# Spectral gate beside a feed-forward block: the opening as one written-out list, and three real products per complex product in half of the transform over s

## The chip, the cores and the metric

One core of a Trainium2 chip runs the whole program. The metric is device time in microseconds, the median of several executions. PE is TensorE (matmuls), PEld its weight loads, DVE VectorE, ACT ScalarE, POOL GpSimd, SP SyncE, whose queue issues most DMAs.

## What is computed

```python
def reference(A_x, A_w_r, A_w_i, B_x, B_w1, B_w2):      # x: 1 x 2048 x 1024
    xn = _layernorm(A_x, axis=-1)
    X = jnp.fft.rfft2(xn, axes=(-2, -1)) * (A_w_r + 1j * A_w_i)
    s = jnp.fft.irfft2(X, s=(2048, 1024), axes=(-2, -1))
    h = _silu(xn @ B_w1)                                 # 1024 x 3584
    g = _silu(h @ B_w2)                                  # 3584 x 1024
    return A_x + s * g
```

Two parts share the normalized input: a feed-forward block of two large products, and a two-dimensional Fourier transform with a filter in the frequency domain. The last line joins them.

## The kernel before

Everything that goes through PE is float32 split into two float16 halves, `hi` and `lo`, and a product is the sum of three: hi x hi, hi x lo, lo x hi. The high half is an ACT copy (`high`, line 253) and the low half a DVE subtraction (`low`, line 256).

**The first FFN product** (`mm1`, line 449) makes, for a block `c` of 512 positions (four blocks) and a tile `f` of 128 hidden columns (28 tiles), 24 matmuls of 512 columns into one PSUM tile of the tag "ff" (four of them). Its stationary operand is the weight tile `w1t[f]`, its moving operand the transposed normalized block `xnT[c]`. Before a weight tile can be used it is loaded (`load`), its largest absolute value per row taken (`maxi`), those summed over the partitions by a tiny matmul (`column_sums`, line 260), a power of two derived from the sum (`scales`), and the halves made (`split`, `rest`). The weight tiles 0 and 1 share one sum, and so do 2 and 3.

**The second FFN product** (`mm2`, line 537) runs as seven products `m` of block sums and differences, each in eight steps `j`; a step is 42 matmuls of 512 columns (9 us).

**The spectral part** is done between these, as background. `ln_gen` normalizes and transposes; block 0 by matmuls (`trans`), the others by transposing DMAs (`entering`, `turned`). `fa_mat` and `fd_gen` transform along the model dimension and do the first radix-4 steps along positions; the results, real and imaginary planes `v`, go to DRAM as `vd`, split in halves (`high_r`, `low_r`). `f_gen` (line 935) then runs 16 units `u`, with `q = u // 4` and `j = u % 4`. For each unit PE multiplies the planes by cosine and sine matrices `kq` (`mat`, line 958): with cosine 128x256 on both planes, with sine and minus sine 128x128 crosswise, for four `c` and three halves each, 36 matmuls into one PSUM tile of the tag "ft" (two of them). ACT copies half of it (`copy`, line 984), DVE forms sum and difference straight from PSUM (lines 1015 and 1016), does a radix-4 step, multiplies with the filter (1030, 1031, 1043, 1044) and does the radix steps of the inverse (1047 to 1066, a small share on POOL). The result is split (`high_z`, `low_z`) and stored as `zd` when four units are done; the tile `zq` is then taken again, so the high half after it waits for that store. `edge_gen` (line 1074) does the same for the one column left over: 12 POOL copies (1089 to 1092), 18 tiny float32 matmuls into a tile "eps" (1096 to 1098), small POOL products. `i_gen` transforms back (1215, 1223, 1305) and writes the rows of `s` (last at 1352) that `finish_out` uses.

**The order.** Each engine works its instructions in the order in which this program issues them. After each half of a product step, `work` (line 1458) takes up to three steps of the background queue `bg` as long as a count of DVE time, kept by `meter` from instruction sizes, is not more than 1 us ahead of the same count for PE. A generator's `yield` ends a step. The edge job stands in that queue behind the 16 units, and behind it the switch to the inverse transform. The opening is ordered by hand: `WARM` gives numbers of idle matmuls (`spin`) between the steps, and the strings `ENTRY` say, for the first five products, after which third of the matmuls how many steps of which queue are issued (`w` weights, `b` background, `f` and `e` the transform matmuls and evacuations of block 0).

Of the kernel before, what the change touches and what calls it, by code (L numbers as in the profile page):

```python
# [2 lines left out]

# [6 lines left out]
F16 = mybir.dt.float16  # L10
# [12 lines left out]
WARM = [35, 8, 0, 8, 0, 8, 12, 0, 0, 0, 0]  # L23
LEAD, PAUSE, LAST = 1.0, -1, 6
IORDER = (1, 3, 0, 2)
SUMMED = (4, 5)
TURNED = (2, 3)
EXTRA = (20, 22, 24)
ENTRY = ("fbwb||ew", "bbbwwbb|bwbb|f", "fwwbbw|wbbb|wb", "|wew|wf", "w||w")
# [15 lines left out]
def make_constants():  # L45
# [16 lines left out]
    k = np.stack([-np.sin(th), np.cos(th), np.sin(th)], 3)  # L62
    kc = np.stack(_halves(k, 2.0**14), 3).reshape(4, 128, 3072)
# [65 lines left out]
def spectral_ffn(ctx, tc, x, w_r, w_i, w1, w2, ca, kc, ci, tw, pm, out):  # L129
# [19 lines left out]
    vd = [dp.tile([128, 4, 4, 2, 256], F16, name=f"vd{j}") for j in range(4)]  # L149
    zd = [dp.tile([128, 4, 2, 1024], F16, name=f"zd{c}") for c in range(4)]  # L150
# [96 lines left out]
    e1, m1, r1, rs, s1 = (small(k, NFT) for k in ("e1", "m1", "r1", "rs1", "s1"))  # L247
# [10 lines left out]
    m1b = sm.tile([128, NFT], BF16, name="m1b")  # L258

    def column_sums(name, m, n, ones=ones):  # L260
        ps = pf.tile([128, 512], F32, name=name, tag="ff")
        nc.tensor.matmul(ps[:, 0:n], ones, m, start=True, stop=True)
        return ps[:, 0:n]

    def weights1():
# [11 lines left out]
        def maxi(i):  # L277
            nc.vector.tensor_reduce((m1 if i < 6 else m1b)[:, i:i + 1], raw[i], axis=AX.XY, op=OP.max, apply_absolute_value=True)

        def scales(i, k):  # L280
            sl = slice(i, i + k)
            ps = column_sums(f"s1_{i}", *((m1[:, sl], k) if i < 6 else (m1b[:, sl], k, unit)))
# [21 lines left out]
        for i in range(3):  # L304
            load(i)
        yield 0

        def first(i):

            maxi(i)  # L310
            if i == 0:
                load(3)

        def whole(i):

            split(i)
            if i in (1, 3):
                load(4 + i // 2)

        steps = {"m": first, "s": lambda i: scales(i, 1), "p": lambda i: scales(i, 2), "h": whole, "l": rest}  # L320
        for k in "m0 m1 p0 h0 l0 h1 l1 m2 m3 p2 h2 l2 h3 l3 m4 s4 h4 l4 m5 s5 h5 l5".split():
            steps[k[0]](int(k[1]))
            yield 0
# [125 lines left out]
    def mm1(c, f, between={}):  # L449
        ps = pf.tile([128, 512], F32, name=f"pa{c}_{f}", tag="ff")  # L450
        w, xt = w1t[f], xnT[c]
# [3 lines left out]
        for n, (d, wh, xh) in enumerate(terms):  # L455
            if n in between:
                between[n]()
            nc.tensor.matmul(ps, w[:, wh, d], xt[:, xh, d], start=(n == 0), stop=(n == 23))  # L458
# [238 lines left out]
    def entering(c, stats, norm):  # L697
# [23 lines left out]
        steps = {"s": stats, "n": plain, "h": hi, "l": lo}  # L721
        for k in "s0 s1 n0 h0 n1 l0 h1 s2 l1 s3 n2 h2 n3 l2 h3 l3".split():
            steps[k[0]](int(k[1]))
            yield 0

    def ln_gen(c):
# [33 lines left out]
        if c == 0:  # L760
            for p in range(2):
                stats(p)
                norm[p]()
            trans(0)
            hi(0)
            stats(2)
            norm[2]()
            trans(1)
            hi(1)
            stats(3)  # L770
            norm[3]()
            lo(0)
            yield 0
            trans(2)
            hi(2)
            lo(1)
            yield 0
            trans(3)
            hi(3)
            lo(2)  # L780
            yield 0
            lo(3)
            yield 0
            return
        yield from (turned if c in TURNED else entering)(c, stats, norm)
# [20 lines left out]
    def fd_gen(c):  # L806
# [62 lines left out]
        o, sp = {}, {}  # L869

        def high_r(j):
            sp[j] = ap.tile([128, 4, 2, 256], F16, name=f"Rs{c}_{j}", tag="Rs", bufs=2)
            nc.scalar.activation(sp[j][:, :, 0], o[j], AF.Copy, scale=2.0**-21)

        def low_r(j):
            nc.vector.scalar_tensor_tensor(sp[j][:, :, 1], o[j], 2.0**-21, sp[j][:, :, 0], op0=OP.mult, op1=OP.subtract)
            defer(2, lambda: nc.sync.dma_start(vd[j][:, :, c], sp[j]))

        for j in range(4):
# [11 lines left out]
            o[j] = r.rearrange("a (q r) k -> a q (r k)", r=2)  # L891
            yield 3.9
# [36 lines left out]
    def open_f():  # L929
        J["p"] = ctx.enter_context(tc.tile_pool(name="jit", bufs=1, side="right"))  # L930
        B["es"] = ExitStack()
        B["p"] = B["es"].enter_context(tc.tile_pool(name="flt", bufs=1, side="right"))
        B["k"], B["v"], B["w"], B["z"] = {}, {}, {}, {}

    def f_gen():
# [12 lines left out]

        def load_w(u):
# [8 lines left out]
        def mat(u):  # L958
            q = u // 4
            ps = pt.tile([128, 4, 2, 128], F32, name=f"fx{u}", tag="ft")  # L960
            v, k = B["v"].pop(u), B["k"][q]
# [22 lines left out]
        def copy(u):  # L984
            cps[u] = bp.tile([128, 2, 256], F32, name=f"xc{u}", tag="xc", bufs=1)
# [21 lines left out]
        for u in range(16):  # L1007
# [3 lines left out]
            ps, cpy = psx.pop(u), cps.pop(u)  # L1011
            pv = ps.rearrange("m c r k -> m c (r k)")
            b = bp.tile([128, 2, 2, 128], F32, name=f"xb{u}", tag="xb", bufs=1)
            d = bp.tile([128, 2, 2, 128], F32, name=f"xd{u}", tag="xd", bufs=1)
            tt(b.rearrange("m c r k -> m c (r k)"), pv[:, 0:2], cpy, op=OP.add)
            tt(d.rearrange("m c r k -> m c (r k)"), pv[:, 0:2], cpy, op=OP.subtract)
# [5 lines left out]
            i_, n_, q_ = u // 8, u // 4 % 2, u % 4  # L1022
# [623 lines left out]
```

## Time and profile before

| | |
|---|---|
| median of 3 runs | 1229.07 us (1228.78, 1229.07, 1231.65) |
| the profiled execution | 1231.15 us, its span 1229.4 us |
| matmuls | 6992, each with a weight load |
| PE busy | 1218.5 us, 99% of the span |
| DVE busy | 999.7 us, 81% |
| ACT busy | 471.5 us, 38% |
| first matmul of the first FFN product | at 19.06 us |
| units of `f_gen` | about 570 to 840 us |
| inverse transform's first matmul | at 892.34 us |

A timeline row gives the start, the duration, engine, line, operation, what it writes and reads, the shape and a count of merged instructions; in brackets stands how long the engine had been idle and what ended that. A matmul's duration contains its latency: 512 columns show as 0.38 us but follow one another every 0.216 us. A row of the waits gives who waited for whom, total, times and longest, in us. A row of one tile or line gives shortest, median and longest duration in ns and the first and last start.

### The profile page before, as it was taken

What the parts mean: (1) busy time and instruction counts of PE and PEld (TensorE: products, weight loads), DVE (VectorE), ACT (ScalarE), POOL (GpSimd) and SP (SyncE); (2) the same over time, 40 slices, a digit from 0 to 9 for tenths busy, and PEclk for the clock granted to TensorE, in tenths of its full rate; (3) what the DMA queues carried; (4) which work ended last, traced back from release to release, by engine and by line L of the source; (5) the groups of instructions that cost most, each with busy time, mean ns of one, the idle gap of its engine ahead of it and who ended that gap; (6) DMA issues with size and microseconds to landing.
All of it is one profiled execution on the core that took longest, in us unless ns stands there. A gap on an engine that the chain in (4) does not pass through costs nothing.

```text
span 1229.4 us, 19034 instructions
## 1 busy us (share of the span) xinstructions
PE 1218.5 (99%) x6992; PEld 619.8 (50%) x6992; DVE 999.7 (81%) x1974; ACT 471.5 (38%) x614; POOL 119.7 (10%) x247
## 2 busy tenths in 40 slices
PE   8999999999999999999999999999999999999998
PEld 5544445444544454445445555544455545555545
DVE  7778998799899889887969899885186678798885
ACT  6675343343554555435433222122032222233212
POOL 3320000000000000010001121114111111000000
PEclk9999999999999999999999999999999999999999
DMA  8887477645669797759899989987979999998686
GB/s 250 186 199 182 139 235 218 202 131 166 201 188 299 226 296 225 217 188 285 178 301 236 299 249 192 276 243 244 285 195 286 276 291 331 305 355 327 199 268 253
DMA packets 279550, 295.77 MB, mean 241 GB/s; under 512 B 48544, under 2 KB 207264, under 8 KB 279072
## 3 DMA queue, kind: packets, MB, share of 16 engines
q1 hardware_dynamic: 259440, 235.76, 65.6%
q10 hardware_dynamic: 15984, 51.45, 12.2%
q0 software_dynamic: 4032, 7.34, 3.5%
q8 instruction: 55, 0.90, 0.3%
q14 instruction: 39, 0.32, 0.1%
HBM read 185.95 MB, written 102.25 MB: 234 GB/s over the span
## 4 chain that ended last, share of the span: by engine, by line
PE 70%; DVE 11%; DMA 8%; issue 3%; ACT 3%; POOL 0%; SPq 0%; ACTq 0%; DVEq 0%; POOLq 0%
PE pa L458 41%; PE pb L541 8%; PE pb L543 8%; PE pb L542 8%; DVE Z L1066 2%; DMA zd<-zq 2%; PE id L1305 2%; DVE T L1031 1%; ACT xp L740 1%; DMA sd<-s 1%; DVE w L256 1%; PE iu L1215 1%; DMA ht<-hd_sum_d 1%; DMA wq<-in_A_w_i_dram 1%; DVE zq L997 1%
## 5 line engine op out<-in xcount | busy, mean ns | idle before, releaser
L458 PE MATMUL pa<-xnT,w 128*128 128x512 f16 x2688 | 584.1, 379 | 1.2 <-ACT w L253 0.7
L458 PEld LDWEIGHTS <-w 128*128 128x128 f16 x2688 | 261.4, 98 | 313.1 <-issue 1.2
L541 PE MATMUL pb<-w,ht 128*128 128x512 f16 (+2 forms) x812 | 301.2, 373 | 0.0
L543 PE MATMUL pb<-w,ht 128*128 128x512 f16 (+2 forms) x812 | 301.0, 373 | 0.0
L542 PE MATMUL pb<-w,ht 128*128 128x512 f16 (+2 forms) x812 | 301.0, 372 | 0.0
L543 PEld LDWEIGHTS <-ht 128*128 128x128 f16 x812 | 79.6, 98 | 91.5 <-issue 0.8
L542 PEld LDWEIGHTS <-ht 128*128 128x128 f16 x812 | 79.6, 98 | 87.1 <-issue 0.8
L541 PEld LDWEIGHTS <-ht 128*128 128x128 f16 x812 | 79.6, 98 | 87.0 <-issue 0.6
L467 ACT ACTIVATE h<-pa,s 128x512 f32<-128x512 f32 x112 | 75.8, 678 | 117.6 <-PE pa L458 94.1
L253 ACT ACTIVATE w<-jr,sc 128x512 f16<-128x512 f32 x98 | 68.1, 713 | 84.4 <-DMA jr<-in_B_w_dram 35.9
L253 ACT ACTIVATE hosum<-hr,hs 128x1536 f16<-128x1536 f32 x28 | 44.1, 1574 | 78.3 <-DVE hr L497 41.4
L256 DVE SCALAR_TENSOR_TENSOR w<-jr,sc,w 128x512 f16<-128x512 f32 x98 | 71.1, 744 | 2.7 <-ACT w L253 2.7
L253 ACT ACTIVATE hoone<-h,hs 128x2048 f16<-128x2048 f32 x28 | 56.0, 1999 | 44.6 <-issue 26.5
L256 DVE SCALAR_TENSOR_TENSOR hoone<-h,hs,hoone 128x2048 f16<-128x2048 f32 x28 | 65.6, 2344 | 7.1 <-ACT hoone L253 7.1
L992 ACT ACTIVATE zq<-Z,zs 128x1024 f16<-128x1024 f32 x16 | 18.4, 1148 | 99.1 <-DVE Z L1066 50.9
L256 DVE SCALAR_TENSOR_TENSOR hosum<-hr,hs,hosum 128x1536 f16<-128x1536 f32 x28 | 50.8, 1813 | 2.5 <-ACT hosum L253 2.5
L496 DVE TENSOR_TENSOR hr<-h 128x1024 f32<-128x1024 f32 x28 | 34.2, 1222 | 22.8 <-ACT h L467 22.8
L634 ACT ACTIVATE pl<-pl,c 128x512 f32<-128x512 f32 (+2 forms) x28 | 17.4, 656 | 67.9 <-DVE pl L610 39.1
L965 PE MATMUL fx<-vq,kq 128*128 128x256 f16 x192 | 43.2, 273 | 0.0
L253 ACT ACTIVATE w<-w1r,rs 128x1024 f16<-128x1024 f32 x28 | 31.9, 1144 | 29.0 <-DVE w L256 19.1
L966 PE MATMUL fx<-vq,kq 128*128 128x128 f16 x192 | 42.0, 219 | 0.0
L967 PE MATMUL fx<-vq,kq 128*128 128x128 f16 x192 | 42.0, 219 | 0.0
(225 smaller groups left out, 1514.0 us busy)
## 6 DMA issues: line engine op xcount, KB each, us to landing
w1r<-in_B_w_dram SPq DMA_DIRECT2D x28, 512.0 KB, 6.5
hd_sum<-hosum SPq DMA_DIRECT2D x56, 256.0 KB, 2.9
hd_one<-hoone SPq DMA_DIRECT2D x56, 256.0 KB, 3.7
hd_dif<-hoone SPq DMA_DIRECT2D x56, 256.0 KB, 3.2
w2m<-in_B_w_dram SPq DMA_DIRECT2D x28, 512.0 KB, 6.2
ht<-hd_dif ACTq DMA_DIRECT2D x32, 448.0 KB, 6.2
jr<-in_B_w_dram SPq DMA_DIRECT2D x56, 256.0 KB, 6.9
ht<-hd_sum ACTq DMA_DIRECT2D x32, 448.0 KB, 5.9
```

The lines of the kernel that those rows point to most:

```text
L253: nc.scalar.activation(hi, raw, AF.Copy, scale=scale)
L256: nc.vector.scalar_tensor_tensor(lo, raw, scale, hi, op0=OP.mult, op1=OP.subtract)
L458: nc.tensor.matmul(ps, w[:, wh, d], xt[:, xh, d], start=(n == 0), stop=(n == 23))
L467: nc.scalar.activation(hq[:, 2 * (c % 2) + f % 2], ps, AF.Silu, scale=s1[:, f:f + 1])
L496: tt(sums[:, 0:2], hq[:, 0::2], hq[:, 1::2], op=OP.subtract)
L541: nc.tensor.matmul(ps, hh[:, 0], w[:, 0], start=first, stop=False)
L542: nc.tensor.matmul(ps, hh[:, 0], w[:, 1], start=False, stop=False)
L543: nc.tensor.matmul(ps, hh[:, 1], w[:, 0], start=False, stop=last)
L965: nc.tensor.matmul(o, k[:, c, kh, 1], v[:, c, vh], start=(n == 0), stop=False)
L966: nc.tensor.matmul(ps[:, c, 0], k[:, c, kh, 2], v[:, c, vh, 128:256], start=False, stop=False)
L967: nc.tensor.matmul(ps[:, c, 1], k[:, c, kh, 0], v[:, c, vh, 0:128], start=False, stop=(n == 2))
L1066: eng.tensor_tensor(Z[:, ns, pos], x0[:, :, ls], x1[:, :, ls], op=o_)
```

## The change

1. The opening is one list of operations by name. `S N T H L` are the statistics, normalization, transposes and halves of block 0's four parts, `A B X Y` the same for block 1, `M s C h l` a weight tile's maximum, column sum, scale and halves, `W` idle matmuls, `f e` transform matmuls and evacuations, `v` a first product's evacuation. `P` and `Q` mark the points within the products up to which the list is issued. The weight tiles 0 to 3 get a sum and scale each; all sums use the bfloat16 matrix. Weight tile 0 is loaded ahead of the third and fourth x tile.
2. The very first product is made in two halves of 256 columns, first the one that needs parts 0 and 1 of the block only.
3. For `q` in (2, 3), the units 8 to 15, a complex product is three real ones: cos (vr + vi), (sin - cos) vi and (-sin - cos) vr, 36 matmuls of 128 columns. `fd_gen` makes and stores the sums vr + vi. The unit's result lies in two "ft" tiles; ACT copies the common product twice over (both planes) and DVE adds the other two to it.
4. The edge job is run inside the units: its loads two a unit from the first unit on, its copies behind unit 13, its matmuls in unit 14, in an "ff" tile.

```diff
-WARM = [35, 8, 0, 8, 0, 8, 12, 0, 0, 0, 0]
+WARM = 35
+THREE = (2, 3)
-ENTRY = ("fbwb||ew", "bbbwwbb|bwbb|f", "fwwbbw|wbbb|wb", "|wew|wf", "w||w")
+ENTRY = (
+    "S0 S1 M0 N0 s0 N1 C0 S2 h0 T0 H0 S3 L0 T1 W12 H1 L1 N2 T2 W4 N3 T3 H2 H3 l0 P0ah A0 L2 L3 P0ax M1 "
+    "P0al P0b0 B0 f0 A1 X0 s1 P0b1 f1 C1 M3 e0 P0b2 M2 f2 h1 A2 s3 s2 v0e B1 Y0 C2 e1 X1 h2 P1b0 l1 P1b1 "
+    "f3 B2 P1b2 C3 P2b0 Y1 P2b1 A3 l2 h3 X2 Y2 P2b2 B3 l3 P3b0 M4 s4 X3 Y3 C4 v1e h4 v2e P3b1 P3b2 v3e Q0 "
+    "Q1 l4 Q2 "
+)
...
+    k[list(THREE)] = np.stack([np.cos(th), np.sin(th) - np.cos(th), -np.sin(th) - np.cos(th)], 3)[list(THREE)]
...
     def mm1(c, f, between={}):
+        parts = ((0, 256), (256, 512)) if c + f == 0 else ((0, 512),)
...
+        for b, (first, stop) in enumerate(parts):
+            for n, (d, wh, xh) in enumerate(terms):
+                if 24 * b + n in between:
+                    between[24 * b + n]()
+                nc.tensor.matmul(
+                    ps[:, first:stop], w[:, wh, d], xt[:, xh, d, first:stop], start=(n == 0), stop=(n == 23))
...
+            both[j] = ap.tile([128, len(THREE), 2, 128], F16, name=f"vt{c}_{j}", tag="wd", bufs=3)
+            nc.scalar.activation(both[j][:, :, 0], total[j], AF.Copy, scale=2.0**-21)
...
+            nc.vector.scalar_tensor_tensor(both[j][:, :, 1], total[j], 2.0**-21, both[j][:, :, 0], op0=OP.mult, op1=OP.subtract)
+            defer(2, lambda: nc.sync.dma_start(vs[j][:, :, c], both[j]))
...
+            nc.vector.tensor_tensor(total[j], some[:, :, 0:128], some[:, :, 128:256], op=OP.add)
+            clock["dve"] -= 0.8
...
         def mat(u):
+            if q in THREE:
+                t_ = B["s"].pop(u)
+                for half in range(2):
+                    ps = pt.tile([128, 2, 512], F32, name=f"fx{u}_{half}", tag="ft")
+                    for i, c in enumerate((half, half + 2)):
+                        for g, src in enumerate((t_[:, c], v[:, c, :, 128:256], v[:, c, :, 0:128])):
+                            for n, (kh, vh) in enumerate(((0, 0), (0, 1), (1, 0))):
+                                nc.tensor.matmul(ps[:, i, 128 * g:128 * g + 128], k[:, c, kh, g], src[:, vh], start=(n == 0), stop=(n == 2))
+                    psx[u, half] = ps
+                return
...
         def copy(u):
+            if u // 4 in THREE:
+                cps[u] = bp.tile([128, 2, 2, 2, 128], F32, name=f"xo{u}", tag="T1", bufs=1)
+                for half in range(2):
+                    nc.scalar.activation(cps[u][:, half], psx[u, half][:, :, 0:128].unsqueeze(2).broadcast_to([128, 2, 2, 128]), AF.Copy)
+                return
...
+            if q in THREE:
+                for half in range(2):
+                    planes = psx.pop((u, half))[:, :, 128:384].rearrange("m i (r k) -> m i r k", r=2)
+                    tt(cpy[:, half], cpy[:, half], planes, op=OP.add)
+                pv = cpy.rearrange("m h i r k -> m i h (r k)")
+                pv, cpy = pv[:, 0], pv[:, 1]
...
+            if u == 12:
+                B["edge"] = edge_gen()
...
+            if u > 12:
+                next(B["edge"], None)
...
-        ps = pt.tile([128, 1024], F32, name="eps", tag="ft")
+        ps = pf.tile([128, 512], F32, name="eps", tag="ff")
...
-                add(bg, edge_gen())
```

Lines 1028 to 1062 of the old loop got `next(B["edge"])` at further steps of units 12 to 15, one step of the edge job each. The filter weights, the number of units and the inverse transform are the same.

216 lines of the change are left out of this document (115 added, 101 removed).

## The prediction

> **What bounds the kernel now.** I read the page's busy line first, then the busy time by stretch, then TensorE's (PE's) waits, and then the timeline wherever one of those three showed a hole.
>
> ```profile
> PE 1218.5 (99%) x6992; PEld 619.8 (50%) x6992; DVE 999.7 (81%) x1974; ACT 471.5 (38%) x614; POOL 119.7 (10%) x247
> ```
> ```profile
> 45.00:1224.70 1179.70, 1178.01 (x6709) 593.85 (x6706) 962.40 (x1908) 438.76 (x582) 105.40 (x209) 1.00 0.82 241
> ```
> ```profile
> PE eps L1096 <- POOL edge L1089: 0.7, 1, 0.7
> PE eps L1098 <- POOL edge L1092: 0.2, 1, 0.2
> ```
>
> The second view's columns are the stretch, its length, then busy time of PE, PEld (weight load), DVE (VectorE), ACT (ScalarE) and POOL (GpSimd), granted clock, DMA share, GB/s. Its stretch from 45 us to 1224.7 us has PE busy 1178.01 of 1179.70 us, so the span is a start, a solid block of matmuls and a short tail. The third view shows all that PE waits for between 560 and 850 us, the spectral units among it: the small edge product, 0.9 us. So a change can win only by streaming fewer columns, by starting the first product sooner, or by mending the edge product; and it loses whatever new wait it gives PE. That DVE is 81% busy costs nothing until PE has to wait for it.
>
> **The units' matrices.** A unit's transform before, and narrow matmuls elsewhere:
>
> ```profile
> 700.00 0.27 PE L965 MATMUL fx<-vq,kq 128*128 128x256 f16 x1
> 700.11 0.22 PE L966 MATMUL fx<-vq,kq 128*128 128x128 f16 x1
> ...
> 702.65 0.38 PE L541 MATMUL pb<-w,ht 128*128 128x512 f16 x1
> ```
> ```profile
> 892.34 2.84 PE L1215 MATMUL iu<-kk,zt 128*128 128x128 f16 x48
> ```
> ```profile
> 22.14 5.34 PE L458 MATMUL pa<-xnT,w 128*128 128x512 f16 x24
> ```
>
> One unit holds PE from 700.00 to 702.65, 2.65 us for 36 matmuls (12 of 256 columns, 24 of 128). After the change it is 36 of 128 columns, each still with its own weight load. What such a stream costs is in the second row: 48 in 2.84 us, the last one's 0.22 being latency, so 2.62 / 47 = 55.7 ns each. 36 x 55.7 ns = 2.01 us; saved 0.64 a unit, and 8 units give **-5.1 us**, all on PE and so all on the path.
>
> Against this change speaks the Trainium skill, "TensorE: Matmul & The Clock Gate", section "Back-to-back issue gap": in a real stream of weight load and matmul it has a 128-column matmul cost some 81 ns, not the isolated 56. By that a unit would take an estimated 2.92 us and the eight units would cost 2.1 us more than now. The trace doesn't bear it out: its 48 narrow matmuls, each with a load, run at 55.7 ns.
>
> The first product in halves is 48 matmuls of 256 columns in place of 24 of 512. By the 0.11 us from 700.00 to 700.11 they take 5.28 us, against (5.34 - 0.38) / 23 = 0.216, so 5.18 us: **+0.1 us**. Fewer warm-up matmuls save nothing by themselves, as they only fill time in which PE has no data.
>
> **The opening.** ACT, DVE, SP (SyncE's queue) and PE:
>
> ```profile
> 7.72 2.58 ACT L740 ACTIVATE x<-x,v 128x1024 f32<-128x1024 f32 x2 [5.50 <-POOL v L739]
> 10.21 1.02 ACT L753 ACTIVATE xnT<-tp 128x1024 f16<-128x1024 f32 x1
> ...
> 17.86 2.19 ACT L253 ACTIVATE w<-w1r,rs 128x1024 f16<-128x1024 f32 x2 [0.77 <-DVE rs L286]
> ```
> ```profile
> 12.41 1.21 DVE L278 TENSOR_REDUCE m<-w1r 128x1 f32<-128x1024 f32 x1
> ...
> 17.06 0.16 DVE L283 TENSOR_SCALAR e<-s 128x2 int32<-128x2 int32 x1
> ```
> ```profile
> 3.07 6.54 SPq L275 DMA_DIRECT2D w1r<-in_B_w_dram  x3
> ```
> ```profile
> DMA to landing us min/median/max: 8.5/9.6/10.1
> ```
> ```profile
> 14.90 1.13 PE L749 MATMUL tp<-ident,x 128*128 128x128 f32 x8 [0.25 <-DVE xnT L757]
> ...
> 19.06 1.90 PE L458 MATMUL pa<-xnT,w 128*128 128x512 f16 x8 [0.71 <-ACT w L253]
> ```
>
> The first product starts at 19.06, released by the first weight tile's high half, which ACT could begin only at 17.86: the scale, whose first step is the 17.06 row, came out of two maxima and a joint column sum. The weight tile itself landed at 3.07 + 8.5 = 11.6. In the new list it is loaded ahead of the third and fourth x tile, and its maximum, sum and scale are taken alone. One tile earlier by two transfers (the three weight tiles land some 1.8 us apart) is 8.6 or so; 1.21 of maximum and about 1.1 of sum and scale give 10.9. From there ACT is the chain: high half 1.1 (2.19 for two), two xnT tiles 2.0, two normalizations 2.6, so 16.6; the last tile's transposes, 1.1 in the 14.90 row, are ahead of the product on PE, and two hand-overs, hence a start near 18.0: **-1.1 us**. Bounds: if the two later x tiles' statistics set it, ACT waits about a microsecond and nothing is won; with no wait for DMA at all ACT has no gap and it is -2. The pieces behind (second scale, second high half, transposes of the second x block) each have a transform or a half product ahead of them on PE; I leave **+0.4** for a wait among the column sums, which stand on PE behind DVE's maxima, with 0 and 1.5 as ends.
>
> **The edge product.** Now it runs alone behind the last unit:
>
> ```profile
> 836.95 0.38 PE L543 MATMUL pb<-w,ht 128*128 128x512 f16 x1
> 838.01 0.40 PE L1096 MATMUL eps<-edge,perm 128*128 128x24 f32 x2 [0.68 <-POOL edge L1089]
> ...
> 840.13 0.38 PE L1096 MATMUL eps<-edge,perm 128*128 128x24 f32 x2
> ...
> 840.80 0.38 PE L541 MATMUL pb<-w,ht 128*128 128x512 f16 x1
> ...
> 842.01 0.63 PE L542 MATMUL pb<-w,ht 128*128 128x512 f16 x1
> 842.44 0.63 PE L543 MATMUL pb<-w,ht 128*128 128x512 f16 x1
> ```
> ```profile
> 700.00:840.00 140.00, 139.01 (x861) 75.41 (x860) 128.70 (x237) 29.85 (x42) 24.61 (x52) 1.00 0.89 233
> 840.00:890.00 50.00, 50.00 (x229) 22.81 (x230) 12.20 (x18) 7.54 (x12) 14.15 (x43) 0.97 0.99 290
> ```
>
> PE was due at 837.17 and is back on the main product at 840.80: 3.63 us. The last six matmuls, with nothing to wait for, take 0.67, so 18 take 2.0 and 1.6 are waits for POOL's 12 copies. Then matmuls of 512 columns come 0.43 us apart instead of 0.216, and the stretch from 840 to 890 has a granted clock of 0.97, which over 50 us is some 3 us at half speed: 1.6 us more. The change issues the copies behind unit 13 and the matmuls two slots later, in unit 14. If the copies are done by then, 1.6 is won; whether the half clock comes all the same I take as even, 0.8: **-2.4 us**. Ends: -3.2 with both gone, and +3.4 where PE waits for unit 13 to finish (first rival). The Trainium skill's section "Part 1: The HAM clock gate" in the same page says that the clock is judged in free-running windows of 3.4 us; the 0.43 us spacing agrees with its half rate. By that, 2.0 us of tiny matmuls without a wait would seldom fill a window.
>
> **What DVE, ACT and the tiles get.**
>
> ```profile
> DVE zq L997 <- ACT zq L992: 14.4, 3, 8.5
> ```
> ```profile
> L1016 DVE TENSOR_TENSOR xd<-fx,xc 128x512 f32<-128x512 f32 x10 | 6.8, 676 | 0.0
> ```
> ```profile
> 811.85 0.27 PE L965 MATMUL fx<-vq,kq 128*128 128x256 f16 x1
> ```
> ```profile
> 813.22 0.68 DVE L1016 TENSOR_TENSOR xd<-fx,xc 128x512 f32<-128x512 f32 x1
> ```
> ```profile
> L1352 DVE SCALAR_TENSOR_TENSOR rows<-sk,spa x4: 282/283/285, 1166.3 to 1191.7; 128x128 f32<-128x128 f32 x4
> ```
> ```profile
> L876 DVE SCALAR_TENSOR_TENSOR Rs<-Ro,Rs x16: 1212/1218/1226, 155.9 to 547.5; 128x1024 f16<-128x1024 f32 x16
> ```
>
> Each changed unit has two more adds of 128x512: 2 x 0.68 = 1.36 us, 10.9 in all; ACT copies twice instead of once. In the forward part 16 steps get an add and a split of 256 elements: by a quarter of 1.218 at least, by half of 0.676 plus an issue at most, 0.6 to 0.9 together, about 13 us spread over 400; there the diff takes 0.8 us back from the planner's count, so the order stays as it is and DVE's idle fifth takes it. Neither is on PE. The planner counts the unit's adds (its meter sees every DVE instruction), so units come out further apart and the last ones move into 840 to 890, where DVE works 12.2 of 50 us; the edge steps that stood there now ride inside the units. The inverse transform's last rows are at 1191.7 and their last use is the final product, which ends at 1224.7: 33 us of cover for a delay of at most 24. If that cover were gone, the tail would grow by the excess. The new 128 KB stores and 256 KB loads are issued two units ahead like their neighbours; the small edge loads go two per unit in the first eight on SP's queue, in front of those units' weight loads, and the permutation's load moves from unit 14 to 12. On POOL the edge's copies and small sums now stand among the Z steps of units 13 to 15, for which ACT's high halves wait; a delay there reaches DVE, not PE, and falls in the idle stretch.
>
> What is new for PE is the PSUM tile. Before, a unit took one of the two "ft" tiles, so its matrix had a whole unit's grace. Now a unit takes both, and the next unit's matrix waits until DVE's two adds have read them. The last unit shows how near that is: its matrix starts at 811.85, while DVE finishes reading the unit before at 813.90. The adds stand ahead of that reading and would release the tiles some 0.7 us earlier, so this one would have waited 1.4 us. Seven such hand-overs; lower end 0, upper end in the second rival. I take **+1.0**, one late hand-over like this one, since only this unit comes behind DVE's 8.5 us wait. ACT's copies for the next unit write the buffer that DVE's last product of this unit still reads, so they come later than now; DVE's eight Z steps cover them. The edge product's tile is one of the four of the main product, free again after ACT's next copy. Behind a waiting matrix stands the whole second FFN product, so such a wait is paid in full.
>
> **Sum:** -5.1 + 0.1 - 1.1 + 0.4 - 2.4 + 1.0 = -7.1 us. The profiled execution took 1231.15 us (span 1229.4), 2.1 above the median of 1229.07; part of that may be its half clock, so against the median I count the clock's 0.8 as nothing: 1229.07 - 6.3 = **1222.8 us**.
>
> **Rivals.** First, the edge product waits. Unit 13 is where DVE lost 8.5 us to ACT's high half (the zq row); POOL's copies stand behind that unit's last step, and PE's edge matmuls only two slots on. A wait of 5 us with the half clock behind it turns -2.4 into +3.4: 1228.6, no change. For it: the same lag is in the 811.85 row. Against it: with units further apart the store that ACT waits for has longer to land. 13 in 100. Second, DVE becomes the bound of the eight units: 128.7 busy, 10.9 more and 14.4 of waits make 154 of 140 us. If PE pays those 14 at the PSUM hand-overs in place of 1, the sum is +6 and the time 1235, slower. It decides from 8 us of waits on, 1.1 a hand-over. Against it: the planner's spacing and the idle DVE behind 840. 6 in 100. A milder form, 4 to 6 us, gives 1226 to 1228: 9 in 100. Third, the change doesn't do what it says on PE: narrow matmuls bound by their loads, at the 81 ns of the page weighed above or worse, a gain of 5.1 turned into a loss; worked from rows it needs over 74 ns (2.65 / 36) and would give 1228 or more. The 892.34 row is against it: 2 in 100. Fourth, the opening gives nothing: 1224.2, inside my range.
>
> **Numbers.** A measurement here tells 0.3%, 3.7 us, from no change. My forecast and the fourth rival, 1219 to 1225, 60 in 100; better still, with no late hand-over and no half clock, 7; no change by the first rival, the milder second or several small losses, 25; slower, 8. The range leaves out about 5 below and 9 above: 1218.5 to 1229.0.
>
> **What would show it.** Right: unit matrices 8 to 15 of 2.0 us; the first "pa" matmul near 18.0; no POOL wait ahead of "eps"; "fx" hardly waiting for DVE; DVE near full to about 850. Wrong: PE idle ahead of "fx" over 5 us in all, an "eps" wait over 3 us, a granted clock of half during the first product, or a last "rows" line beyond 1224.

## The result, and the profile after

The changed kernel takes 1269.76 us (median of 6 runs, 1265.8 to 1276.05), the kernel before beside it 1232.14 (6 runs): ratio 1.0308, 95% interval 1.0272 to 1.0344. It is 3.1% slower where 0.5% faster was forecast. The profiled execution took 1276.05 us, its span 1274.3; it is the slowest of the six, so its trace shows more loss than the medians do (44.9 us against 37.6).

First the page's busy line, then what PE waited for in the whole span (who for whom, total, times, longest):

```profile
PE 1222.8 (96%) x6994; PEld 622.5 (49%) x6994; DVE 1021.8 (80%) x2030; ACT 478.8 (38%) x638; POOL 124.8 (10%) x249
```
```profile
PE pa L469 <- DMA xnT<-xs: 10.7, 2, 8.9
PE fa L782 <- ACT L L792: 10.4, 1, 10.4
PE pa L469 <- ACT h L479: 6.6, 3, 4.7
PE eps L1138 <- POOL edge L1131: 3.8, 1, 3.8
PE iu L1266 <- DVE ub L1275: 3.8, 1, 3.8
PE s L271 <- DVE m L289: 3.7, 1, 3.7
PE pb L553 <- DMA ht<-hd_dif: 3.1, 1, 3.1
PE fx L971 <- DVE xo L1033: 2.2, 1, 2.2
PE fx L971 <- ACT zq L1010: 1.3, 1, 1.3
```

PE's share fell from 99 to 96%. (The wait at `s`, a column sum, ends at 10.4 us, well ahead of the first product.) Counting 0.4218 ns a column (0.216 us for 512; 0.02 us for the tiny ones), the columns of all matmuls take 1197.5 us here and 1204.9 before, 7.4 us less: 5.2 in the units and 2.2 because the opening has 51 idle matmuls in place of 71. What lies between the starts of successive matmuls beyond that (waits and half clock) grew from 18.6 to 70.9 us: 52.3 us lost. 52.3 - 7.4 = 44.9, the difference of the two profiled executions. I call it **excess** below. By hundreds of us it lies ahead of 100 (12.0, before 9.6), behind 100 (11.4, before 0.7), at 400 to 600 (20.6, before 0.2), 700 to 900 (17.8, before 5.5) and behind 1000 (8.3, before 1.7).

The busy time of some stretches of the kernel after, columns as in the prediction (stretch, length, PE, PEld, DVE, ACT, POOL, granted clock, DMA share, GB/s):

```profile
95.00:120.00 25.00, 16.10 (x65) 6.69 (x63) 16.72 (x38) 14.75 (x13) 0.11 (x1) 0.80 0.72 160
440.00:480.00 40.00, 27.67 (x175) 15.16 (x174) 31.56 (x51) 23.92 (x33) 0.64 (x5) 0.87 0.83 258
575.00:600.00 25.00, 20.33 (x89) 8.81 (x87) 17.01 (x27) 10.50 (x14) 1.39 (x1) 0.93 0.98 305
840.00:890.00 50.00, 46.21 (x257) 24.56 (x256) 42.32 (x74) 12.76 (x19) 22.20 (x57) 0.90 0.70 212
```

In each of these stretches PE's row has a hole and the granted clock is under 1. There a wait is paid twice, once as idle time and once in the half clock behind it: behind the wait that ends at 112.3 us ten matmuls of 512 columns follow one another every 0.43 us in place of 0.216. Not every wait has it: between 700 and 840 us PE waits 1.3, 2.2 and 3.1 us, and the granted clock there is 1.00. DVE works 42.3 us between 840 and 890 where it worked 12.2 before, but mostly because the units begin 31 us later; in the kernel before it works 36.9 us between 809 and 859.

Where the forecast's own marks are concerned, the first product and the matrices of unit 9 in PE's timeline:

```profile
18.10 3.66 PE L469 MATMUL pa<-xnT,w 128*128 128x256 f16 x32
...
760.16 0.33 PE L971 MATMUL fx<-vs,kq 128*128 128x128 f16 x3
...
762.17 0.38 PE L553 MATMUL pb<-w,ht 128*128 128x512 f16 x1
```

The product starts at 18.10, and a unit's 36 matmuls take 762.17 - 760.16 = 2.01 us. Both are what was forecast. (The start varies: over the twelve kernels here that have the new list it lies between 17.1 and 19.1 us, middle 18.0; over the eight with the old one between 19.0 and 20.4.) The time went elsewhere.

### The profile page after: what moved, and what is told of

The parts are those of the page before. It is cut to its first block, busy times and chain, and to the rows that moved or that the text cites. A ratio compares the mean times of both kernels' runs of the same rounds, so it can differ in the third digit from the quotient of the medians.

```text
span 1274.3 us, 19144 instructions
## 1 busy us (share of the span) xinstructions
PE 1222.8 (96%) x6994; PEld 622.5 (49%) x6994; DVE 1021.8 (80%) x2030; ACT 478.8 (38%) x638; POOL 124.8 (10%) x249
## 4 chain that ended last, share of the span: by engine, by line
PE 31%; DVE 22%; DMA 16%; issue 3%; SPq 3%; ACT 2%; POOL 0%; ACTq 0%; DVEq 0%
PE pb L553 7%; PE pb L554 7%; PE pb L555 7%; PE pa L469 5%; DMA w1r<-in_B_w_dram 2%; DMA ht<-hd_dif 2%; DVE hoone L265 2%; DMA zd<-zq 2%; DMA sd<-s 2%; DVE wd L384 2%; DMA vs<-vt 2%; DMA jr<-in_B_w_dram 1%; PE id L1348 1%; SPq L502 1%; DMA out_dram<-pl 1%
## 5 line engine op out<-in xcount | busy, mean ns | idle before, releaser
L469 PE MATMUL pa<-xnT,w 128*128 128x512 f16 (+1 forms) x2712 | 588.4, 379 | 17.3 <-DMA xnT<-xs 10.7
L469 PEld LDWEIGHTS <-w 128*128 128x128 f16 x2712 | 264.5, 98 | 330.6 <-issue 24.1
L265 DVE SCALAR_TENSOR_TENSOR hoone<-h,hs,hoone 128x2048 f16<-128x2048 f32 x28 | 65.7, 2345 | 10.3 <-ACT hoone L262 10.2
L289 DVE TENSOR_REDUCE m<-w1r 128x1 bf16<-128x1024 f32 x28 | 33.9, 1215 | 21.4 <-DMA w1r<-in_B_w_dram 21.3
L262 ACT ACTIVATE w<-w1r,rs 128x1024 f16<-128x1024 f32 x28 | 32.0, 1143 | 33.3 <-DVE w L265 14.2
L425 POOL DMA_DIRECT2D jr<-in_B_w_dram x28 | 24.5, 922 | 168.9 <-DMA jr<-in_B_w_dram 104.1
L1010 ACT ACTIVATE zq<-Z,zs 128x1024 f16<-128x1024 f32 x16 | 18.4, 1147 | 55.8 <-DVE Z L1101 30.3
L1101 POOL TENSOR_TENSOR Z<-yb 128x32 f32<-128x32 f32 x32 | 16.2, 524 | 218.0 <-DVE yb L1080 161.5
```

Source lines behind the costliest of these rows:

```text
L262: nc.scalar.activation(hi, raw, AF.Copy, scale=scale)
L265: nc.vector.scalar_tensor_tensor(lo, raw, scale, hi, op0=OP.mult, op1=OP.subtract)
L289: nc.vector.tensor_reduce(m1[:, i:i + 1], raw[i], axis=AX.XY, op=OP.max, apply_absolute_value=True)
L425: nc.gpsimd.dma_start(raw[n], w2_block(*todo[n], 1), accum_op=OP.add)
L469: nc.tensor.matmul(ps[:, first:stop], w[:, wh, d], xt[:, xh, d, first:stop], start=(n == 0), stop=(n == 23))
L1010: nc.scalar.activation(zqs[q][:, 0, :, 16 * j:16 * j + 16], zs_[u], AF.Copy, scale=zs)
```

## The experiments

The difference is always to the kernel before, run beside it on the same chip. Three explanations stood at first. *Count*: the added forward work, hidden from the planner by `clock["dve"] -= 0.8`, makes DVE late. *Buffers*: the sums' tiles `vt` share a ring of three with the weight sums `wd`, and ACT waits for a store. *Order*: blocks 2 and 3 are normalized and transposed too late.

**Order: block 2 one step earlier (e3).** SP's queue, kernel before, and after:

```profile
88.31 5.58 SPq L675 DMA_TRANSPOSE xnT<-xs  x4
...
96.73 6.17 SPq L675 DMA_TRANSPOSE xnT<-xs  x4
```
```profile
95.22 16.21 SPq L687 DMA_TRANSPOSE xnT<-xs  x8
```

Block 3's eight transposes went out in two groups, the last by 102.9; now they end at 111.4, and PE waits 8.9 us for them. In the old code `finish(bg, ln[c])` for block 1 ran into the next job of the queue and so issued block 2's first step; the new list has no such call.

```diff
                 until()
+                slot(bg)
                 for _ in range(2):
                     slot(wq)
```


> The changed kernel with one background step more at the end of the opening. In the kernel before, the call that finished block 1's normalization also took the first step of block 2's, at product 4; with the new list that call is gone, and every step of blocks 2 and 3 stands one product (5.2 us) later. Order theory: with the step put back the transposes of block 3 are issued a product earlier, and PE's wait of 9.1 us at 103 us and the half clock behind it (11.4 us of excess there) go, so that product 15 starts at about 102 instead of 112.3; the end moves less than that, if ACT and DVE then lag by as much more at 461 us: 1258 to 1268. Rival: x of block 3 is loaded late, or ACT is the limit with its four normalizations in a row; then the wait stays above 6 us.

1256.05, +27.0 us (ratio 1.0228, 1.0202 to 1.0254), 10.6 less than the change's +37.6. The kernel's queue and its first stretch:

```profile
90.50 5.76 SPq L687 DMA_TRANSPOSE xnT<-xs  x4
...
99.10 6.14 SPq L687 DMA_TRANSPOSE xnT<-xs  x4
```
```profile
95.00:120.00 25.00, 23.44 (x109) 10.57 (x108) 21.48 (x59) 15.41 (x17) 0.23 (x2) 1.00 0.76 181
```

The order theory holds: the wait is gone. The wait at 461 us went too, though others came between 542 and 569 (12.5 us of excess between 500 and 600).

**Buffers: tiles of their own (e1).** In the kernel after, ACT's timeline, and SP's:

```profile
466.12 0.42 ACT L862 ACTIVATE vt<-vt 128x256 f16<-128x256 f32 x1 [14.20 <-DMA vs<-vt]
```
```profile
455.73 0.52 SPq L502 DMA_DIRECT2D hd_one<-hoone  x1
...
460.08 0.70 SPq L870 DMA_DIRECT2D vs<-vt  x1
```

A high half of 0.42 us stands 14.2 us on ACT until the store of an older sum, put off by two products and issued at 460.08 behind others, has landed and freed the buffer. Behind it stand the evacuations, hence `fa` waiting 10.4 us.

```diff
-            both[j] = ap.tile([128, len(THREE), 2, 128], F16, name=f"vt{c}_{j}", tag="wd", bufs=3)
+            both[j] = ap.tile([128, len(THREE), 2, 128], F16, name=f"vt{c}_{j}", tag=("EE", "EO", "P", "Q")[j], bufs=1)
```


> The changed kernel with one edit: the halves of the sums vr + vi (tile vt, line 861) no longer take turns with the weight sums wd in one ring of three buffers; each j has the buffer of a butterfly tile that is idle then. Buffer theory: in the changed kernel ACT stood 14.2 us before a vt high half until the store of an older sum had landed, and 8.6 us before another for a wd, and DVE 4.2 us; PE then stood 10.6 us at 461 us for ACT's evacuation and 4.8 at 580. With buffers of their own PE's waits between 400 and 600 us go (20.6 us of excess over pure streaming in that stretch, half clock included): 1249, or 1.013 of the kernel before. Count theory: the lag comes from some 0.85 us of DVE work in each of 16 steps that the planner does not see; the buffers make no difference and the time stays at 1265 to 1273. Neither touches the wait of 9.1 us at 103 us.

1259.19, +30.1 (1.0241, 1.0226 to 1.0256): 7.5 better, not 20. Excess between 400 and 500 fell from 14.3 to 2.1, but that between 500 and 600 rose from 6.3 to 10.3. The buffers were one cause of two in that stage.

**Count: the forward adds counted (e2).**

```diff
-            clock["dve"] -= 0.8
```


> The changed kernel without the line that takes 0.8 us back from the planner's count of DVE time at each forward step. Count theory: the list again gives DVE no more than it can do, the 10.6 us at 461 us and the 4.8 at 580 go, 1249. Buffer theory: the same tiles in the same ring with the same late stores; ACT still stands over 8 us before a vt high half, 1262 to 1273.

1284.63, +55.6 (1.0456, 1.0421 to 1.0491): 18 us worse. The count theory fell, with the sign turned round:

```profile
565.54 0.42 ACT L862 ACTIVATE vt<-vt 128x256 f16<-128x256 f32 x1 [9.56 <-DVE vt L887]
...
579.91 0.42 ACT L862 ACTIVATE vt<-vt 128x256 f16<-128x256 f32 x1 [3.43 <-DVE vt L887]
...
586.72 0.69 ACT L479 ACTIVATE h<-pa,s 128x512 f32<-128x512 f32 x1 [5.45 <-DMA vs<-vt]
```

The forward stage must be finished at a fixed product. With its steps rationed more strictly more of them are left for that point, the last four radix steps come in a row (four `vt` high halves, the first and last shown), and PE waits 18.0 us in one piece for `h`. The line in the change was needed.

**Both mended (e4).** The first two edits together.

> Both edits of the two other runs: the sums' own buffers and block 2's first step at product 4. If both causes are right and independent: 11.4 and 20.6 us off, 1238, 1.005 of the kernel before; the rest is the smaller waits in the units, at the edge product and at 1097 us. If the late block 3 had only hidden a lag of DVE that is there anyway, the sum is less than the two alone: 1245 or more.

1251.44, +22.4 (1.0182, 1.0160 to 1.0205). Alone the two edits won 10.6 and 7.5 us, together 15.3 of the 18.1; that is far from the 1238 that the excess had promised. 22 us remain that neither explains.

**Chasing single waits (e7 to e11).** Edits that start from e4's kernel. e7 moves the first load of `kq`, which on ACT's queue stands until the last sums' stores have landed, to POOL's queue and begins the units a step later; e8 is e7 with the edge job later. e9 is e4 with that load on SP's queue; e10 is e9 with the edge job back behind the units; e11 is e10 with the matrices later.

```diff
-            nc.scalar.dma_start(t_, kf[q])
+            (nc.scalar if q else nc.gpsimd).dma_start(t_, kf[q])
...
-                f_job = add(bg, switch(A, open_f, 1, max_job))
+                f_job = add(bg, switch(A, open_f, 2, max_job))
```


> The run with own buffers and block 2 early, and two more edits, each with its own place in the trace. First, the load of the first cosine matrices kq goes out on POOL's queue: on ACT's it stood 10.7 us until the last sums' stores had landed (6.0 in the kernel before, behind vd), with the evacuations behind it and PE waiting 5.3 us at 557; that wait and its half clock, 7.9 us, go. Second, the spectral units begin one step later, as they did before block 2's step was moved: the second tile of unit 8's matrices was then 6.3 us late at 718 us, and 1.4 in the changed kernel; 5 to 8 us go there. Together 1238. If the lag of DVE behind PE (10 to 16 us in the units, 6 to 8 in the kernel before) is not a matter of the phase, the wait at unit 8 stays above 4 us: 1244.

```diff
-            if u > 13:
+            if u > 14:
                 next(B["edge"])
             yield 2.3
...
         low_z(15)
+        next(B["edge"], None)
```


> The run before it in this list with the edge product's matmuls one step later in unit 14 (all its later steps too). The wait of 3.7 us for POOL's copies at 831 us and the half clock around it go, some 6 us in all, if a step (5 us) is enough for POOL: 1232. If POOL's copies are late because DVE is late by a whole unit, a step moves the wait little: 1236 to 1238.

```diff
-            nc.scalar.dma_start(t_, kf[q])
+            (nc.scalar if q else nc.sync).dma_start(t_, kf[q])
```


> The run with own buffers and block 2 early (1251.4), with one edit: the first cosine matrices kq are loaded over SP's queue, where the next load (vq) waits for the same stores anyway. On POOL's queue the evacuations were free of the wait but the matrices came 6.6 us late for unit 0. If the queue is what matters: no wait at 557 us and unit 0's matrices in time, 7.9 us off, 1243.5. If the last sums' stores are what both wait for (they landed at 561.8, 4 to 5 us later than the last stores of the kernel before would have), PE waits at unit 0 instead and the time stays near 1250.

```diff
-            for e in range(2 * u, 2 * u + 2):
...
+                add(bg, edge_gen())
```


> The kernel of the run with kq over SP's queue, with the edge job again behind the units, one edge load a unit and its own ft tile, as in the kernel before. Edge theory, narrow: only the wait at eps and the half clock around it change, 10.1 us of excess behind 800 us become the 5.1 of the kernel before, 5 us off. Edge theory, wide: the double rate of tiny edge loads in units 0 to 7 (each pair held the queue some 3 us between landings) is also what makes DVE lag 12 to 15 us behind PE in units 3 to 7, against 3 to 8 in the kernel before; then the lag falls back to 8 and unit 8's wait of 6.5 us for its second tile falls under 2: 10 us off or more.

```diff
-            if u + 1 < 16:
+            if u + 1 < 8:
                 mat(u + 1)
...
             yield 2.5
+            if 8 <= u + 1 < 16:
+                mat(u + 1)
```


> The kernel of the run with the edge job behind, with the matrices of units 8 to 15 issued one step (about 5 us) later, just ahead of ACT's copy of them. If PE's waits at the two-tile hand-over come from a lag of DVE of some 10 to 15 us against a distance of 16 us between units, the waits at units 8 and 11 (6.5 and 1.0 us, with half clock 9.4) go. If DVE is the bound of the stage, DVE then waits for PE and the same time is lost behind the units.

Differences: +24.2 (1.0182 to 1.0224), +25.8 (1.0190 to 1.0223), +24.2 (1.0171 to 1.0214), +21.3 (1.0134 to 1.0191), +23.8 us (1.0170 to 1.0218). All five stay between +21 and +26. Most waits that were aimed at shrank or went, and others took their place; the one at `eps` did not in e10 (3.5 us, 3.0 in e9). The largest wait of PE in the kernels of e7, e10 and e11:

```profile
PE fx L978 <- DMA wq<-in_A_w_r_dram: 6.4, 1, 6.4
```
```profile
PE iu L1249 <- DVE ub L1258: 6.2, 1, 6.2
```
```profile
PE pb L553 <- DMA ht<-hd_dif: 5.9, 2, 3.0
```

With `kq` on another queue unit 0 waits for its loads instead. With the edge job behind (e10 against e9), DVE's sums in unit 3 come 10.2 us after its matrices instead of 15.7; up to there the two kernels differ in the edge loads alone, so in this kernel their double rate cost DVE some 5 us. Unit 8's wait shrank from 8.1 to 2.0, and PE waited in the inverse transform instead. With the matrices later no `fx` of units 8 to 15 waits, and products wait for their loads. Mending one wait at a time showed nothing more, so I took the change apart.

**The two halves, each alone on the kernel before (e5, e6).**

```diff
-WARM = [35, 8, 0, 8, 0, 8, 12, 0, 0, 0, 0]
+WARM = 35
...
+        parts = ((0, 256), (256, 512)) if c + f == 0 else ((0, 512),)
```


> The kernel before with the first half of the change alone: the opening as one list, the first product in halves; units, forward steps and edge job as before. If the halves of the change add up: the late steps of blocks 2 and 3 cost the 11.4 us seen behind 103 us, and the opening itself ends where it did (+0.3 at product 4), so 1229 + 12 = 1241. Rival: without the sums' work in the forward steps DVE and ACT have no lag then and the transposes come in time, 1229 to 1232.

```diff
+THREE = (2, 3)
...
+            if u == 12:
+                B["edge"] = edge_gen()
```


> The kernel before with the second half of the change alone: three real products in units 8 to 15, sums made and stored in the forward steps in the ring of three buffers, edge job inside the units; opening as before. If the halves add up: 38 us less the opening's 12, that is 1255. From the run with block 2 a step earlier, 1256 less the opening's own +0.3, the same. If the ring's waits grow only when block 3 is late, less: 1245.

Opening +13.9 (1.0110, 1.0087 to 1.0133), the rest +24.6 (1.0198, 1.0183 to 1.0213): together 38.4 against 37.6. The halves add up. Then four kernels before with one part each, sums (e12), units (e13), edge job (e14), and the opening with block 2's step put back (e15). e13 takes the real plane in the place of the sum, so no sums are made, stored or loaded there:

```diff
+            both[j] = ap.tile([128, len(THREE), 2, 128], F16, name=f"vt{c}_{j}", tag="wd", bufs=3)
...
+            defer(2, lambda: nc.sync.dma_start(vs[j][:, :, c], both[j]))
...
+            clock["dve"] -= 0.8
```


> The kernel before with the sums vr + vi made, split and stored in the forward steps exactly as in the change (same ring, same count), and read by nobody. Forward theory: PE's waits at 539 to 561 us and the half clock behind them, 12.7 us of excess in the run with the second half alone, come from these steps, so 1229.5 + 12 = 1242, and units of the kernel before then wait little. If the forward part also sets the lag of DVE in the units, more: 1245. If DVE's idle fifth hides them, as forecast: 1230.

```diff
+                        for g, src in enumerate((v[:, c, :, 0:128], v[:, c, :, 128:256], v[:, c, :, 0:128])):
...
+                    tt(cpy[:, half], cpy[:, half], planes, op=OP.add)
```


> The kernel before with three real products in units 8 to 15 (two tiles, ACT's copy, DVE's two adds), with the real plane in the place of the sum, so that no sums are made, stored or loaded; its output is not the reference's for that. Forecast's terms: 5 us less streaming, 1 us of hand-over, 1225. DVE theory (second rival): two adds of 0.68 us in each of 8 units on an engine that is busy 128.7 of 140 us make PE wait 14 at the hand-overs and behind, 1229.5 - 5 + 14 = 1238. Inherited lag theory: the hand-over waits only because DVE comes late out of the forward stage, then 1224 to 1227.

```diff
+            if u == 12:
+                B["edge"] = edge_gen()
...
-                add(bg, edge_gen())
```


> The kernel before with the edge job inside the units alone: loads two a unit from unit 0, copies behind unit 13, matmuls in unit 14. Forecast's term: 2.4 us less, 1227. First rival: PE waits some 3 to 4 us at eps with the half clock behind it, and the tiny loads put 2 to 5 us on DVE's lag in units 3 to 8 without PE waiting, 1230 to 1233.

```diff
                 until()
+                slot(bg)
```


> The kernel before with the opening as one list and the first step of block 2 back at product 4. If the late step was all that the opening cost: 1243.3 less 11.5 to 13.9, that is 1229.5 to 1232; the opening's own 1.1 us are given back at 44 us, where PE waits 1.9 for block 1's last transpose and runs at half clock behind it. If it brought in more than that: over 1234.

Sums +11.8 (1.0102, 1.0083 to 1.0121); units +2.7 (1.0016, 0.9998 to 1.0034, no difference that can be told); edge job +4.7 (1.0042, 1.0024 to 1.0061); mended opening +3.4 (1.0037, 1.0020 to 1.0055). So the late step of block 2 is 13.9 - 3.4 = 10.4. Such a difference of two comparisons is good to some 3.5 us. In e13 none of the three expectations (1224 to 1227, 1225, 1238) came true. Sums, units and edge make 19.3 of the 24.6; the other 5 appear only together, and are little more than the noise of four comparisons. With all three PE waits at `fx`, with the units alone it doesn't. Two things may stand behind that and were not told apart: DVE comes later to unit 7 (16.5 us behind the start of its matrices, 10.6 to 11.4 with any one part), and the loads of the sums in the units are in none of the single parts. PE's waits in e6, and those in e13 from 560 us on:

```profile
PE fx L986 <- ACT zq L1025: 5.0, 1, 5.0
...
PE fx L986 <- DMA vs<-vs: 1.1, 1, 1.1
```
```profile
PE iu L1246 <- DVE ub L1255: 7.7, 1, 7.7
PE iu L1238 <- POOL zt L1207: 1.5, 1, 1.5
```

And e13's busy time in the units and in the inverse transform, with the latter stretch of the kernel before:

```profile
700.00:840.00 140.00, 140.00 (x888) 73.56 (x887) 138.72 (x249) 37.01 (x53) 17.64 (x38) 1.00 0.92 245
...
1040.00:1070.00 30.00, 22.34 (x148) 12.74 (x147) 19.00 (x42) 6.07 (x12) 0.86 (x1) 0.89 0.95 322
```
```profile
1040.00:1070.00 30.00, 29.77 (x200) 15.92 (x199) 21.03 (x46) 6.07 (x12) 0.86 (x1) 1.00 0.92 310
```

In the units DVE is busy 138.72 of 140 us and PE all 140: the two adds did go into DVE's idle time, and PE's columns fell from 1204.9 to 1199.7 us. The units end later (the last `zq` at 844.3 against 839.9). Then PE waits 7.7 us for `ub` up to 1059, with half clock behind it. DVE's rows there, kernel before and e13, with what PE waited for `ub` before:

```profile
1056.35 0.69 DVE L598 TENSOR_TENSOR pl<-pl,pb 128x512 f32<-128x512 f32 x1 [3.67 <-DMA pl<-pd]
...
1058.17 0.68 DVE L1232 TENSOR_TENSOR ub<-iu,uc 128x512 f32<-128x512 f32 x1
```
```profile
PE iu L1223 <- DVE ub L1232: 0.2, 1, 0.2
```
```profile
1055.24 0.69 DVE L600 TENSOR_TENSOR pl<-pl,pb 128x512 f32<-128x512 f32 x1 [3.58 <-DMA pl<-pd]
1057.51 0.69 DVE L601 TENSOR_TENSOR pl<-pl,pb 128x512 f32<-128x512 f32 x1 [1.58 <-DMA pl<-pd]
...
1058.71 0.68 DVE L1255 TENSOR_TENSOR ub<-iu,uc 128x512 f32<-128x512 f32 x1
```

`ub` comes only 0.5 us later than before. PE begins this part of the inverse transform 6.8 us sooner (1044.4 against 1051.2), by what it saved until then, and has to wait for nearly the same moment. The kernel before already waited there, 0.2 us, so nothing was to spare. DVE is not short of time (19.00 of 30 us busy, 21.03 before); in both kernels it stands ahead of `ub` until loads of `pl` have landed.

**Three questions on the parts (e16, e17, e18).** The sums in buffers of their own, the edge job a step later, and the units with the inverse transform a step later:

```diff
-            both[j] = ap.tile([128, len(THREE), 2, 128], F16, name=f"vt{c}_{j}", tag="wd", bufs=3)
+            both[j] = ap.tile([128, len(THREE), 2, 128], F16, name=f"vt{c}_{j}", tag=("EE", "EO", "P", "Q")[j], bufs=1)
```


> The kernel before with the sums made, split and stored, but in buffers of their own. Ring theory: with the ring ACT stood 13.2 us at 523 to 536 us until an older sum's store had landed, and 8.6 before that for a wd; both go, and with them most of the 12.3 us of excess in 500 to 600: 1231 to 1234. Work theory: the added 13 us of DVE and the stores themselves make DVE and ACT late at the forced end of the forward stage; 1238 or more.

```diff
-            if u > 13:
+            if u > 14:
                 next(B["edge"])
             yield 2.3
```


> The kernel before with the edge job inside the units, its matmuls and all later steps one step later. The prediction's condition: with the copies done by then PE no longer waits (4.3 us) nor runs at half clock at eps, and the job costs less than behind the units: 1228 to 1230. If POOL's copies are a whole unit late, the wait stays above 2 us: 1232 to 1235.

```diff
-                add(bg, switch(B, open_i, 6, lag=2))
+                add(bg, switch(B, open_i, 7, lag=2))
```


> The kernel with the units' three products alone (real plane in the place of the sum, so its output is not the reference's), with one idle step more ahead of the inverse transform. Phase theory: PE's wait of 7.7 us at 1051 us for DVE's ub, and the 1.7 at 897 for the edge copies, come from where the inverse transform's steps fall beside the loads and stores of the products; moved by a step they shrink by half or more, and the units' 5 us show: 1224 to 1228. Load theory: DVE is simply later by the added 10.9 us through the whole stage; the wait stays within 2 us, 1231 to 1234.

The sums: +6.4 (1.0051, 1.0029 to 1.0072), so the ring was some 5.4 of the 11.8. What is left stands in one place, ACT's rows there, kernel before and e16:

```profile
553.02 0.39 ACTq L940 DMA_DIRECT2D kq<-in_kc_dram  x1
553.46 0.69 ACT L467 ACTIVATE h<-pa,s 128x512 f32<-128x512 f32 x1 [6.01 <-DMA vd<-Rs]
```
```profile
560.72 0.39 ACTq L950 DMA_DIRECT2D kq<-in_kc_dram  x1
561.16 0.69 ACT L469 ACTIVATE h<-pa,s 128x512 f32<-128x512 f32 x1 [10.75 <-DMA vs<-vt]
```

At the end of the forward stage all stores that were put off go out together, now with the sums' behind them. The load of `kq` on ACT's queue, into the memory that they leave, waits for the last sum, and the evacuation behind it starts after 10.75 us of idle ACT (6.01 before the change). Both theories were half right.

The edge job: -0.4 (1.0006, 0.9985 to 1.0026), no difference. PE no longer waits at `eps`, and the granted clock there is 1.00; e14's wait, and e17's stretches:

```profile
PE eps L1143 <- POOL edge L1136: 4.3, 1, 4.3
```
```profile
700.00:840.00 140.00, 140.00 (x873) 76.38 (x871) 131.63 (x244) 32.89 (x46) 37.63 (x87) 1.00 0.92 241
840.00:890.00 50.00, 50.00 (x286) 24.79 (x284) 15.72 (x33) 7.72 (x12) 5.75 (x7) 1.00 1.04 286
```

The units with the inverse transform later: +13.3 (1.0103, 1.0069 to 1.0137), 10.6 worse than without the delay. Both expectations fell; the waits grew:

```profile
PE iu L1246 <- DVE ub L1255: 10.3, 1, 10.3
PE id L1328 <- DVE sk L1342: 4.3, 1, 4.3
```

One idle step is half a product step, some 4.5 us, and cost 10.6, more than in full. The two profiled executions differ by 14.0 us; 9.4 of them lie between 1000 and 1100, and 4.1 between 800 and 900, where PE now waits 1.8 us at `eps`. No kernel here beats the one before by more than can be told.

## Why the prediction was wrong, step by step

**Units' matrices, -5.1: right as streaming time.** 2.01 us a unit against 2.01, 5.2 us of columns less with the units alone. The Trainium skill's 81 ns for a narrow matmul with its load ("TensorE: Matmul & The Clock Gate", "Back-to-back issue gap") did not come about: 36 in 2.01 us are 55.8 ns each. **First product in halves, +0.1: right**, 32 rows in 3.66 us. **PSUM hand-over, +1.0: right in kind only.** With the units alone there is none; in the whole change 2.2 + 1.3 us, where DVE arrives later.

**"All on PE and so all on the path": failed.** The saved columns did not shorten the kernel: the units alone cost 2.7 us (-0.2 to +4.2). 200 us behind the units PE needs DVE's `ub`, which waits for loads that come no sooner. PE already waited 0.2 us there before the change, so what PE saves ahead of it turns into a wait: 7.7 us with the units alone. That this point bounds every saving ahead of it is read from these two traces; no run moved those loads.

**The opening, -1.1 + 0.4: failed, the largest miss.** Its start was forecast to 0.1 us. The gain was given back within 28 us: PE waited 1.8 us for block 1's last transpose and product 4 began at 46.3 in place of 46.0. (The +0.4 for column sums did not come; their one wait lies ahead of the first product.) And the forecast priced the list up to its end only. That the old call also issued a step of the job behind it, and so set when block 3 was ready 60 us later, was in the code and was not looked at: 10.4 us. The forecast put no term there. Of the 3.4 us that the opening costs with that step put back, e15's trace (its slowest execution) shows 2.1 us of waiting for block 1's last transpose with a granted clock of 0.92 between 40 and 62 us, and 0.7 and 1.6 us for ACT's evacuations ahead of 104 us.

**"Neither is on PE": failed for the forward part.** The 13 us of DVE work (13.5 measured) were indeed hidden. What was missed is the tile: the prediction asked what the added instructions cost and not whose buffer they write and when that is given back. A 0.42 us copy waited 14.2 us for a late store; with the sums alone this ring costs some 5.4 us, the later end of the stores 6.4. The prediction had put the whole at nothing.

**Edge product, -2.4: its condition failed.** The copies were not done by then; the first rival's wait came (3.8 us, 4.3 alone), and the part alone costs 4.7. One step later the wait and the half clock are gone, and nothing measurable is won. The wait that this term meant to save was no fixed cost either: with the edge job behind the units as before, PE does not wait at `eps` at all in e5, e12, e13 and e16.

**"33 us of cover for a delay of at most 24": looked in the wrong place.** It compared the last rows with their last use. The inverse transform waits for DVE long before that, at `ub`, where there was no cover at all. The second rival (DVE as the bound of the units, paid by PE) is not borne out by the units alone: DVE was near full there and PE did not wait. No rival named order or buffers, where the two largest causes lie.

The parts: late block 2 10.4, opening else 3.4, sums 11.8 (ring 5.4, last stores 6.4), edge 4.7, units 2.7, and some 5 where they meet: 38 of 37.6. Forecast for the opening, the sums, the edge and the units with their hand-over were -0.6, 0, -2.4 and -4.1. Without block 2's late step and the ring the parts make 22.5, and e4 has +22.4. Not settled is why every further edit of e4's kernel left +21 to +26. That the transfers leave PE no room in the units and the inverse transform would explain it; it is argued from the traces, not shown.

## What to carry to other kernels

Before an engine's idle share is called cover, ask for each added instruction whose buffer it writes, which store frees that, and how late that store is issued: on an engine that works in order, a copy of 0.4 us can hold it for 14. When hand-ordered code is rewritten, list everything that the old calls issued as a side effect, above all steps of the jobs behind, and follow each to its last user. A saving in one stage counts only if the next points at which the engine waits for another have been looked at, in the middle and not just at the tail: a wait of 0.2 us in the profile before marks a point at which nothing is to spare.

## What was not expected of the hardware

Waits of 9 to 10 us each had a granted clock well under 1 about them (0.80 over the 25 us from 95 on, 0.87 over the 40 from 440 on), so that the 8.9 us at 103 cost 11.4; the three waits of up to 3.1 us between 700 and 840 left it at 1.00. Tiny loads are not free: in e9's kernel pairs of edge loads of 2 KB stood among the transfers, and moving them apart took DVE's lag in unit 3 from 15.7 to 10.2 us. In the kernel before the same pairs (e14, e17) cost that lag only 1.6 and 2.1 us, so the price is not a fixed one.
